# Attention and a SwiGLU feed-forward block on one core: preparing head pair 13 next to pair 12

## The chip, the core and the metric

The kernel runs on one core of a Trainium2 chip. The core has a matrix engine (TensorE, PE in the profile), a vector engine (VectorE, DVE), a scalar engine for activations (ScalarE, ACT), a general engine (GpSimd, POOL) and a queue engine (SyncE, SP), each with its own stream of instructions, and 16 DMA engines that all of them share. The metric is the time of one execution on the device, in microseconds (us); lower is better. The profile comes from one execution that was recorded.

## The reference

Softmax attention over 8 batches of 12 heads, sequence 448, head size 64, and behind it a feed-forward block on the 3584 tokens of width 768, with an inner width of 1536:

```python
scores = scale * np.matmul(q, k.transpose(0, 1, 3, 2))
attn = exp(scores - max) / (sum + 1e-09)
x = np.matmul(attn, v).transpose(0, 2, 1, 3).reshape(B * S, H * D)
g, val = x @ w_gate, x @ w_val
out = (g * sigmoid(g) * val) @ w_out
```

## The kernel before

**Pairs.** The attention is worked in 48 pairs of heads, six to a batch; two heads of 64 fill TensorE's 128 rows. A pair needs q and k with the head dimension on the partitions. Pairs 0 to 10 are transposed by TensorE. From pair NPE = 11 on, the float16 copies of q and k are laid side by side in a tile `qk16` by POOL, and a DMA transpose that SP issues writes them to `qkT`. From pair FULL = 12 on, the key rows are cut in three chunks of 128 and a remainder of 64 per head, so that the score matmuls use all 128 columns. `prep` (its branch for `pr >= FULL`, lines 188 to 203) does this for one pair: two memsets for the padding (L193, L194), a copy of the main k rows (L195), two of the remainder rows (L197), one of q (L198), and the transpose on SP (L200). There are three `qk16` buffers and five of `qkT`.

**Loads.** `load_qk16` issues the loads of q and k from POOL's queue, which also converts float32 to float16. With `n=2` it loads two pairs, with `n=1` one. From pair 12 on that is four DMAs: q (L127), main k rows (L136), and the remainder rows of each head (L138, twice). Pairs 12 and 13 are loaded together by the entry ("qk", 12) of the work queue `wq`, under pair 4. From pair 14 on each pair is loaded when the pair six before it (LA = 6) is entered. V is loaded in groups of three pairs: `load_v` with a memset (L165), two remainder loads (L167) and a main load (L171) for part 0, and one main load for the others. The gate and value weights (L185), and w_out in two halves (`wo`, L187, 1152 KB each), come through POOL's queue as well. The two halves of w_out are issued when pairs 6 and 7 are entered. All these DMAs take turns with eight completion semaphores: the ninth waits for the first to land.

**Order of work.** The order is written out by hand and each engine follows it. The main loop runs over visits. A visit issues the scores of two or three chunks (`qk`, TensorE matmul L275 and exponential L278 on ScalarE); from pair 12 on, a visit is one pair. Then it prepares a later pair: when pair `pr` is entered, `prep(pr + 3)` is called, and after it `load_qk16(pr + 6, 1)`. Then come the sums or the weighted values of an earlier pair (`reduce4`, L299), the V load of a later group, and a share of the feed-forward work: gate and value products (L362 or L365, in four column tiles when `tiled`), activation L381, the two vector steps L393 and L396, out-products (`op<-wo,hts`) and their copy L426. The remainder scores of a pair (`qk_rest`, tile `sr`) end its visit. The first out-products, those of the first feed-forward block, use the first half of w_out for its three row chunks and then the second half for the same chunks.

Around the change the visits go: pair 9 is entered, then pair 10 (within the next visit), pair 11, and from pair 12 on one pair per visit. So pair 12 is prepared under pair 9, pair 13 under pair 10, pair 14 under pair 11 and pair 15 under pair 12. Pair 14 is loaded under pair 8, pair 15 under pair 9, pair 16 under pair 10.

Of the kernel before, what the change touches and what calls it, by code (L numbers as in the profile page):

```python
# [19 lines left out]
NPE = 11  # L20
# [4 lines left out]
FULL = 12  # L25
# [3 lines left out]
def kernel(  # L29
# [19 lines left out]
    NPAIR = B * NHP  # L49
# [139 lines left out]
    def prep(pr):  # L189
        if pr >= FULL:  # L190
            rq, km, kr = raw[pr]
            qk16 = attp.tile([128, 2, NC, 2, D], FP16, tag="qk16", bufs=3, name="qk16")
            nc.gpsimd.memset(qk16[96:128, 1], 0.0)  # L193
            nc.gpsimd.memset(qk16[:, 0, 3], 0.0)  # L194
            nc.gpsimd.tensor_copy(qk16[:, 0, 0:3].rearrange("p c h d -> p h c d"), km)  # L195
            for hx in range(2):
                nc.gpsimd.tensor_copy(qk16[ts(hx, SR), 0, 3, hx], kr[ts(hx, SR)])  # L197
            nc.gpsimd.tensor_copy(qk16[0:P, 1].rearrange("p c h d -> p h c d"), rq)  # L198
            qkT[pr] = attp.tile([128, 2 * NC, 128], FP16, tag="qkT", name="qkT", bufs=5)
            nc.sync.dma_start_transpose(  # L200
                qkT[pr][:], qk16[:].rearrange("p t c h d -> p (t c h d)")
            )
            return None
        rq, rk = raw[pr]
        if pr == 0 or pr >= NPE:
            qk16 = attp.tile([128, 2, NC, 2, D], FP16, tag="qk16", bufs=3, name="qk16")[0:P]
            for t, src in enumerate((rq, rk)):
                dst = qk16[:, 1 - t].rearrange("p c h d -> p h c d")
                if pr == 0:
                    nc.vector.tensor_copy(dst[:, 0], src[:, 0])  # L210
                    nc.scalar.activation(dst[:, 1], src[:, 1], AF.Copy)
                else:
                    nc.gpsimd.tensor_copy(dst, src)
        qkT[pr] = attp.tile([128, 2 * NC, 128], FP16, tag="qkT", name="qkT", bufs=5)
        qkT[pr] = qkT[pr][:].rearrange("p c q -> p (c q)")[:, 0 : 2 * NC * P].rearrange(
            "p (c q) -> p c q", q=P
        )
        if pr >= NPE:
            nc.sync.dma_start_transpose(
                qkT[pr], qk16.rearrange("p t c h d -> p (t c h d)")  # L220
            )
            return None

        def turn0():
            for t in range(2):
                tp = ps_s.tile([128, 2, 512], FP32, tag="s", name="tp")
                for c in range(NC):
                    for hx in range(2):
                        nc.tensor.matmul(
                            tp[ts(hx, 64), c // 2, ds(c % 2 * P, P)],  # L230
                            lhsT=qk16[:, 1 - t, c, hx],
                            rhs=ident[:],
                            start=True,
                            stop=True,
                        )
                dst = qkT[pr][:, ts(1 - t, NC)].rearrange("p (a c) q -> p a (c q)", a=2)
                nc.vector.tensor_copy(dst[:, 0], tp[:, 0, 0 : 2 * P])
                nc.scalar.activation(dst[:, 1], tp[:, 1, 0 : 2 * P], AF.Copy)

        def turn():  # L240
            if pr < FIRST + 2:
                tp = ps_s.tile([128, 2 * NC, 256], FP16, tag="s", name="tp")
            else:
                tp = ps_f.tile([128, 2 * NC, 128], FP16, tag="f", name="tp")
            for t in range(2):
                for c in range(NC):
                    for hx in range(2):
                        src = raw[pr][t][:, hx, c, :]
                        nc.tensor.transpose(tp[ts(hx, 64), (1 - t) * NC + c, 0:P], src, ident[:])
            nc.vector.tensor_copy(qkT[pr], tp[:, :, 0:P])  # L250

        return turn if pr else turn0
# [10 lines left out]
    def qk(pr, c):  # L263
        if c == 0:
            E[pr] = ep.tile([128, 2 * NC * S], FP16, tag="E", name="E")
        t = qkT[pr]
        s = ps_s.tile([128, 2, 512], FP32, tag="s")
        full = pr >= FULL
        for hx in range(2):
            if full:  # L270
                lhsT, rhs = t[ts(hx, 64), c], t[ts(hx, 64), NC:, 0:P]
            else:
                lhsT = t[ts(hx, 64)].rearrange("p c q -> p (c q)")[:, c * P : c * P + 128]
                rhs = t[ts(hx, 64), NC:, :].rearrange("p c q -> p (c q)")
            nc.tensor.matmul(s[:, hx, 0:S], lhsT=lhsT, rhs=rhs, start=True, stop=True)  # L275
        m = 128 if full else P
        dst = (e_main if full else e_old)(pr)[:, c]
        nc.scalar.activation(dst, s[0:m, :, 0:S], AF.Exp, scale=sm_scale)  # L278
# [42 lines left out]
    def scaled(p0, t, acc):  # L321
        b, hp = divmod(p0, NHP)
        kk, bb = divmod(b, NB)
        if kk not in X:
            X[kk] = xp.tile([128, NCB, NB * S], FP16, tag="X", name="X")
        nc.vector.tensor_tensor(  # L326
            X[kk][:, hp + t, ts(bb, S)], acc[:, 0:S], R[p0][:], ALU.mult
        )
# [124 lines left out]
    with tc.manual_schedule():  # L453
# [47 lines left out]
        def add_block(i, visits):  # L501
            f1, f2, n = block(i)
            oq.extend(ffn2_wait)
            ffn2_wait.clear()
            fvq.extend([(f1, NCB * n / 2400.0)] * NFB)
            own = [(f2, NFB * OH / 2400.0)] * (2 * (n // 128))
            (oq if i == 0 else ffn2_wait).extend(own)
            count.update(visits=visits, fv=NFB, o=len(oq), at=0, more=NFB - visits)
# [21 lines left out]
        def run_budget(budget):  # L530
            while (fvq or oq) and budget > 0:
                budget -= run_fv() if fvq else run_o()
            return budget
# [68 lines left out]
        def product(kind, p0):  # L602
            if kind == "sums":
                pop_deferred(99)
                deferred.extend(recips(p0, sums(p0)))
            else:
                if kind == 0:
                    pop_deferred(99)
                scaled(p0, kind, pv(p0, kind))

        carry = 0.0
        for x, (chunks, todo) in enumerate(plan):
            for pr, c in chunks:
                qk(pr, c)
            end = min([y for y in adds if y > x] + [len(plan) + 1])
            if x == 0:
                for t in range(2):
                    scaled(p4, t, halves[t])
                add_block(0, end)
            turn2 = None  # L620
            entered = [pr for pr, c in chunks if c == 0]
            for pr in entered:
                if NPE <= pr + 3 < NPAIR:
                    prep(pr + 3)
                if 14 <= pr + LA < NPAIR:
                    load_qk16(pr + LA, 1)
            for pr, c in chunks:
                if c == 2 and pr < NPE - 2:
                    prep(pr + 2)()
            any_p = len(todo)  # L630
            if x in adds and x > 0:
                while todo:
                    product(*todo.pop(0)[1:])
                add_block(adds[x], end - x)
            while todo:
                product(*todo.pop(0)[1:])
            for pr in entered:
                if 4 <= pr // GP + 1 < NGRP:
                    load_v(pr // GP + 1, pr % GP)
                for w in wq.pop(pr, []):  # L640
                    emit(w)
            tiled[0] = bool(any_p) and (not chunks or chunks[0][0] >= TILED)
            rests.extend(pr for pr in entered if pr >= FULL)
            if adds[max(y for y in adds if y <= x)] < 2:
                carry = run_budget(left() / (end - x) + carry)
            else:
                at, n = count["at"], count["visits"]
                no = share(count["o"], at, n)
                nf = 1
                if no and count["more"] > 0:  # L650
                    o_left = sum(1 for y in range(at, n) if share(count["o"], y, n))
                    extra = -(-count["more"] // o_left)
                    nf += extra
                    count["more"] -= extra
                count["at"] += 1
                for y in range(nf):
                    if fvq:
                        run_fv()
                for _ in range(no):
                    run_o()  # L660
            run_rests()
            tiled[0] = False
# [36 lines left out]
```

## Time and profile before

| what | value |
|---|---|
| median of 6 runs | 460.84 us (460.3 to 462.8) |
| the profiled execution, its own time | 462.8 us |
| its span, first to last instruction | 461.0 us |
| mean granted TensorE clock | 0.993 |
| busy share of the span: PE, DVE, ACT, POOL | 97%, 51%, 50%, 52% |
| moved by DMA | 45.63 MB, 99 GB/s over the span |
| the two halves of w_out, issue to landing | 14.4 and 22.6 us |
| DMA transposes, issue to landing, shortest, median, longest | 3.4, 5.2, 12.2 us |

The page gives busy time by engine, the chain of work that ended last, and groups of instructions by source line. A timeline lists one engine's instructions in order: start, duration, line, tiles, and in brackets the idle time just before with what ended it. In the view of DMA, q0 is the queue of POOL's loads and q1 that of the transfers that SP issues.

### The profile page before, as it was taken

The numbers are of one execution on the slowest core, as the hardware profiler recorded it, in microseconds if no ns is written. First come the engines' busy times: TensorE is split into PE (matmuls) and PEld (weight loads), VectorE is DVE, ScalarE is ACT, GpSimd is POOL, SyncE is SP. The second block draws the span as 40 slices with busy tenths as digits, with TensorE's granted clock in tenths as the row PEclk, the third lists the DMA queues.
The fourth block names the chain that finished last, engine by engine and source line by source line (L and its number), as shares of the span: only waits on it lengthen the run. The fifth ranks groups of instructions, "written<-read, shape, count | busy, mean of one in ns | idle before, by whom it ended". The sixth has DMA issues, their size and how long they took to land.

```text
span 461.0 us, 17413 instructions
## 1 busy us (share of the span) xinstructions
PE 447.9 (97%) x7844; PEld 251.5 (55%) x7844; DVE 236.9 (51%) x375; ACT 231.4 (50%) x353; POOL 237.9 (52%) x472
## 2 busy tenths in 40 slices
PE   8899996999999999999999999999999999999996
PEld 3355554444456666555556656555556667544564
DVE  2765763267764563645636636446456456355200
ACT  6986574555555544544465465445544642222222
POOL 8554707999899979970589609990150000000000
PEclk9999999799999999999999999999999999999999
DMA  9999997897879889973479747973353101200133
GB/s 135 197 200 201 181 181 87 109 182 94 115 96 107 125 114 116 138 97 43 78 103 118 108 83 94 131 82 81 48 67 60 37 3 42 66 0 2 34 104 102
DMA packets 100618, 45.63 MB, mean 99 GB/s; under 512 B 71360, under 2 KB 97088, under 8 KB 100544
## 3 DMA queue, kind: packets, MB, share of 16 engines
q0 software_dynamic: 56320, 23.38, 43.9%
q1 hardware_dynamic: 44128, 21.09, 25.0%
q8 instruction: 61, 1.00, 1.0%
q14 instruction: 13, 0.11, 0.1%
q10 hardware_dynamic: 96, 0.05, 0.0%
HBM read 47.19 MB, written 11.01 MB: 126 GB/s over the span
## 4 chain that ended last, share of the span: by engine, by line
PE 83%; DMA 11%; DVE 1%; POOL 1%; ACT 1%; issue 1%; SPq 0%; DVEq 0%
PE vp L365 18%; PE gp L365 18%; PE op L365 16%; PE acc L299 11%; PE op L362 6%; PE s L275 6%; DMA wo<-in_moe_w_out_dram 5%; PE gp L362 4%; PE vp L362 4%; DMA wg<-in_moe_w_gate_dram 2%; DMA q<-in_q_dram 2%; PE sr L365 1%; DMA qkT<-qk 1%; ACT E L278 1%; DMA rk<-in_k_dram 1%
## 5 line engine op out<-in xcount | busy, mean ns | idle before, releaser
L278 ACT ACTIVATE E<-s 128x896 f16<-128x896 f32 (+1 forms) x156 | 131.6, 923 | 17.1 <-PE s L275 16.8
L365 PE MATMUL gp<-X,wg 128*32 128x384 f16 (+1 forms) x1824 | 99.6, 351 | 0.0
L365 PE MATMUL vp<-X,wv 128*32 128x384 f16 (+1 forms) x1824 | 99.3, 351 | 0.0
L393 DVE SCALAR_TENSOR_TENSOR t<-sg,gp 128x384 f32<-128x384 f32 (+1 forms) x96 | 58.5, 610 | 72.2 <-ACT sg L381 71.6
L365 PE MATMUL op<-wo,hts 128*32 128x384 f16 x1968 | 87.7, 329 | 0.4 <-issue 0.4
L426 ACT ACTIVATE osb<-op 128x384 f32<-128x384 f32 (+1 forms) x57 | 27.7, 486 | 117.9 <-PE op L365 94.2
L381 ACT ACTIVATE sg<-gp 128x384 f32<-128x384 f32 (+1 forms) x96 | 52.6, 547 | 62.6 <-PE gp L365 36.1
L350 DVE RECIPROCAL R<-ssb 128x112 f32<-128x112 f32 x92 | 73.8, 829 | 0.1
L365 PEld LDWEIGHTS <-hts 128*32 128x32 f16 x1968 | 57.1, 98 | 26.5 <-issue 2.4
L365 PEld LDWEIGHTS <-wg 128*32 128x32 f16 x1824 | 51.9, 97 | 35.3 <-issue 0.5
L365 PEld LDWEIGHTS <-wv 128*32 128x32 f16 x1824 | 51.9, 97 | 34.5 <-issue 1.6
L396 DVE SCALAR_TENSOR_TENSOR hts<-t,vp 128x384 f16<-128x384 f32 (+1 forms) x96 | 59.6, 621 | 10.8 <-DVE t L393 1.0
L326 DVE TENSOR_TENSOR X<-acc,R 128x448 f16<-128x448 f32 x48 | 29.7, 624 | 46.0 <-PE acc L299 42.3
L275 PE MATMUL s<-qkT 64*128 64x448 f16 x312 | 41.8, 357 | 7.1 <-DMA qkT<-qk 4.7
L138 POOL DMA_DIRECT2D k<-in_k_dram x70 | 38.2, 558 | 15.6 <-DMA wo<-in_moe_w_out_dram 14.1
L299 PE MATMUL acc<-E,vt 128*32 128x448 f16 (+1 forms) x768 | 45.7, 358 | 0.0
L347 DVE COPY ssb<-acc 128x448 f32<-128x448 f32 x23 | 14.4, 625 | 55.9 <-PE acc L299 55.9
L165 POOL MEMSET vt<- 128x384 f16 x12 | 5.3, 445 | 55.9 <-PE acc L299 55.9
L283 ACT ACTIVATE E<-sr 128x448 f16<-128x448 f32 x36 | 19.6, 544 | 24.7 <-PE sr L365 24.7
L127 POOL DMA_DIRECT2D q<-in_q_dram x42 | 28.6, 681 | 5.4 <-PE s L275 2.5
L299 PEld LDWEIGHTS <-vt 128*32 128x32 f16 (+1 forms) x768 | 18.6, 97 | 20.3 <-issue 8.7
L362 PE MATMUL op<-wo,hts 128*128 128x384 f16 (+1 forms) x192 | 29.6, 316 | 0.0
(53 smaller groups left out, 363.0 us busy)
## 6 DMA issues: line engine op xcount, KB each, us to landing
q<-in_q_dram POOLq DMA_DIRECT2D x37, 112.0 KB, 3.6
vt<-in_v_dram POOLq DMA_DIRECT2D x36, 96.0 KB, 3.4
k<-in_k_dram POOLq DMA_DIRECT2D x34, 96.0 KB, 4.4
out_dram<-osb SPq DMA_DIRECT2D x7, 336.0 KB, 3.2
wg<-in_moe_w_gate_dram POOLq DMA_DIRECT2D x8, 288.0 KB, 11.0
wv<-in_moe_w_val_dram POOLq DMA_DIRECT2D x8, 288.0 KB, 11.2
wo<-in_moe_w_out_dram POOLq DMA_DIRECT2D x2, 1152.0 KB, 18.5
out_dram<-osb SPq DMA_DIRECT2D x8, 288.0 KB, 3.0
```

The costliest lines, as they stand in the source:

```text
L127: nc.gpsimd.dma_start(q16[:, here], qf.rearrange("h (p c) d -> p h (c d)", c=NC))
L138: nc.gpsimd.dma_start(kr[ts(hx, SR), ds(h0 // 2, n)], kf[:, SM:].rearrange("(i t) p d -> t p i d", t=2)[hx],)
L275: nc.tensor.matmul(s[:, hx, 0:S], lhsT=lhsT, rhs=rhs, start=True, stop=True)
L278: nc.scalar.activation(dst, s[0:m, :, 0:S], AF.Exp, scale=sm_scale)
L299: nc.tensor.matmul(acc[ts(j, 32), 0:S], lhsT=weights(pr, hx, c), rhs=rhs, start=(c == 0), stop=(c == NC - 1),)
L326: nc.vector.tensor_tensor(X[kk][:, hp + t, ts(bb, S)], acc[:, 0:S], R[p0][:], ALU.mult)
L350: lambda i=i: nc.vector.reciprocal(rt[:, ts(i, P)], ssb[:, ts(i, P)]) for i in range(4)
L362: nc.tensor.matmul(dst, lhsT=lhsT, rhs=rhs, start=start, stop=stop)
L365: nc.tensor.matmul(dst[ts(j, 32), :], lhsT=lhsT[:, ts(j, 32)], rhs=rhs, start=start, stop=stop)
L381: nc.scalar.activation(sg[:, 0:n], gp[:, 0:n], AF.Tanh, scale=0.5)
L393: nc.vector.scalar_tensor_tensor(t1[:, 0:n], sg[:, 0:n], 1.0, gp[:, 0:n], ALU.add, ALU.mult)
L396: nc.vector.scalar_tensor_tensor(hts[:, fb, 0:n], t1[:, 0:n], 0.5 * HS, vp[:, 0:n], ALU.mult, ALU.mult)
```

## The change

When pair 9 is entered, pair 13 is prepared right behind pair 12, and no longer when pair 10 is entered. The loads of pair 15 follow behind both. Every other pair is prepared where it was. No engine gets an instruction more or less, and the order changes on POOL alone: the two memsets and four copies of pair 13 now stand between the copies of pair 12 and the four loads of pair 15. Before, these four loads and the four instructions of a V load (L165, L167 twice, L171) stood between them. SP's transposes keep their order.

```diff
             for pr in entered:
-                if NPE <= pr + 3 < NPAIR:
+                if NPE <= pr + 3 < NPAIR and pr + 3 != FULL + 1:
                     prep(pr + 3)
+                if pr + 3 == FULL:
+                    prep(FULL + 1)
                 if 14 <= pr + LA < NPAIR:
                     load_qk16(pr + LA, 1)
```

## The prediction

> **What bounds the kernel now.** I read the page first, then TensorE's timeline where its one long wait stands, then the queues behind that wait.
>
> The page (busy shares, the chain of waits, and the group of the wait):
>
> ```profile
> PE 447.9 (97%) x7844; PEld 251.5 (55%) x7844; DVE 236.9 (51%) x375; ACT 231.4 (50%) x353; POOL 237.9 (52%) x472
> ...
> PE 83%; DMA 11%; DVE 1%; POOL 1%; ACT 1%; issue 1%; SPq 0%; DVEq 0%
> ...
> L275 PE MATMUL s<-qkT 64*128 64x448 f16 x312 | 41.8, 357 | 7.1 <-DMA qkT<-qk 4.7
> ```
>
> TensorE (PE) is busy 97% of the span: whatever delays it, or saves it a wait, goes almost whole into the time. The third line names one wait of 4.7 us on a transposed copy. TensorE's timeline (start us, duration us, engine, line) shows it:
>
> ```profile
> 72.73 4.08 PE L365 MATMUL op<-wo,hts 128*32 128x384 f16 x96
> 76.62 0.38 PE L365 MATMUL sr<-qkT 128*32 128x448 f16 x4
> 81.69 1.30 PE L275 MATMUL s<-qkT 64*128 64x448 f16 x6 [4.69 <-DMA qkT<-qk]
> 82.92 1.69 PE L299 MATMUL acc<-E,vt 112*32 112x448 f16 x16
> 84.38 3.16 PE L365 MATMUL op<-wo,hts 128*32 128x384 f16 x48
> 87.37 0.36 PE L365 MATMUL sr<-qkT 128*32 128x448 f16 x4
> 87.67 0.74 PE L275 MATMUL s<-qkT 64*128 64x448 f16 x6
> ```
>
> By the order of the program the scores at 70.39 are pair 12's, at 81.69 pair 13's, at 87.67 pair 14's, at 95.34 pair 15's. Pair 13 is waited for from 77.0 to 81.69. After it the same six score matmuls last 1.30 us against 0.74: TensorE runs at half clock (the clock record has 0.5 from 79.66 for 6.83 us). From 81.69 to 87.67 pass 5.98 us; the same steps at full clock, from their own starts elsewhere (scores 0.67, P·V 0.77, 48 matmuls of the out-product 1.95, remainder scores 0.19), take 3.6. So the stall costs 4.7 + 2.4 = 7.1 us. That is the prize.
>
> POOL's timeline shows why pair 13 is late:
>
> ```profile
> 54.54 0.61 POOL L198 COPY qk<-q 112x512 f16<-112x512 f16 x1
> 55.09 0.67 POOL L127 DMA_DIRECT2D q<-in_q_dram  x1
> 55.75 0.73 POOL L136 DMA_DIRECT2D k<-in_k_dram  x1
> 61.87 0.54 POOL L138 DMA_DIRECT2D k<-in_k_dram  x1 [5.39 <-DMA wo<-in_moe_w_out_dram]
> 71.11 0.53 POOL L138 DMA_DIRECT2D k<-in_k_dram  x1 [8.70 <-DMA wo<-in_moe_w_out_dram]
> ...
> 74.38 0.52 POOL L193 MEMSET qk<- 32x512 f16 x1
> ...
> 76.13 0.61 POOL L198 COPY qk<-q 112x512 f16<-112x512 f16 x1
> ...
> 79.91 0.52 POOL L193 MEMSET qk<- 32x512 f16 x1
> ...
> 81.66 0.61 POOL L198 COPY qk<-q 112x512 f16<-112x512 f16 x1
> ```
>
> Pair 12 is prepared up to 55.1. Then come the four loads of pair 15; the last two reuse semaphores of the two halves of w_out and wait until these have landed (61.55 and 70.83: issued 47.15 and 48.17, landing after 14.4 and 22.6). Pair 13's copies stand behind them at 74.38, pair 14's at 79.91. SP's transposes follow the copies at once: issued 50.38, 55.17, 76.77, 82.30, 87.84 for pairs 11 to 15, landing after 10.5, 12.2, 4.9, 5.0, 5.6 us, so at 60.9, 67.4, 81.65, 87.3, 93.4. Pair 14's lands only 0.4 us before TensorE asks for it at 87.67. That is the next in line.
>
> **What the skill says.** "TensorE: Matmul & The Clock Gate", Part 1: TensorE falls to half clock after an idle window of about 3.4 us and returns after a busy one, the windows running free of the kernel. The trace agrees in size: 6.83 us is two such windows; here a window that still held 0.7 us of work sufficed to drop. "DMA: Bandwidth & Descriptors", Queues, rings and completion order: each DMA engine alternates packet by packet between the queues with work. The trace agrees, 370 packets against 368 below.
>
> **The change, part by part.** Nothing is added or removed. Pair 13's two memsets, four copies and transpose move ahead of the four loads of pair 15.
>
> *Copies, 2.36 us of POOL.* 0.52+0.20+0.50+0.52+0.61 = 2.35, and by the timeline from 74.33 to 76.69. They now run from 55.1 to 57.45. Their data was loaded with pair 12's (issued before 44, and copied from at 53.5 without a wait); the third qk16 buffer is free. The cover is the idle time of 5.39 us before 61.87, which shrinks to 3.0; were it gone, 2.36 us would be added to POOL's queue. Pair 15's first two loads slip 2.36 us, at no cost: they stand behind w_out in POOL's DMA queue and landed at 72.2 and 72.7 anyway, and pair 15 is copied after 85.
>
> *Transpose 13.* Issued at about 57.5, behind transpose 12. Transpose 11 landed at 60.9, 12 at 67.4: 6.4 us each under the weights' load. So 13 lands near 73.8, with 3 us to spare before 77.0. The 4.7 us wait goes.
>
> *What the transpose does to w_out.* DMA view of 68 to 70, with no transpose under way, then of 64 to 66 with transpose 12 (queue: packets, MB, share):
>
> ```profile
> q0 software_dynamic: 799, 0.37, 141.5%
> ```
>
> ```profile
> q0 software_dynamic: 370, 0.28, 90.2%
> q1 hardware_dynamic: 368, 0.09, 35.8%
> ```
>
> The loads drop from 0.37 to 0.28 MB per 2 us, and 62 to 64 has only 0.17, a standstill of nearly 1 us in mid-transpose. In its first 5 us (61 to 66) transpose 12 kept 0.04+0.20+0.09 = 0.33 MB of weights back, 1.8 us at the free rate. Transpose 13 now runs from 67.4, ahead of w_out's last 3.4 us. So w_out's second half lands later by d: 1.2 us without the standstill, 1.8 with it, 3 at the worst; not below 0, for a transpose on the same engines can't speed a load. I take 1.8: landing 72.6, just before TensorE asks at 72.73.
>
> *Pair 14.* Behind that landing POOL's chain is the old one less the copies of pair 13: rest load, memset, V loads, four loads of pair 16, V load, copies of pair 14. Its transpose is issued at 82.30 − 2.36 + d = 79.94 + d and lands 5.0 later: 84.94 + d = 86.7.
>
> *TensorE.* After 77.0 the 3.6 us of pair 13's visit run at full clock, so pair 14 is asked for at 80.6, not at 87.67. It waits from 80.6 to 86.7, 6.1 us instead of 4.7: the stall has not gone, it has moved on by one pair. The clock drops again; half clock costs between 1.2 (restart early in a window) and 2.6 us, 2.4 in this trace; I take 2.0. Pair 14 then begins in effect at 86.7 + 2.0 = 88.7 against 87.67.
>
> *Sum.* −2.36 (copies off POOL's chain) −0.37 (pair 14 had that slack) +1.8 (w_out later) +2.0 (half clock now after pair 14's landing, not ahead of it) = +1.1 us. Against the profiled span of 461.0 that gives 462.1; on the median of 460.84 it gives 461.9. (The profiled execution itself took 462.8, 1.8 over its span; the others 460.3 to 460.94.)
>
> *Next in line.* Pair 15: its transpose goes from 87.84 to about 87.3, landing by 93, asked for at 96. Pair 16's landed at 101.6 for a use at 102.3; POOL is no later and the use is. Nothing further waits.
>
> **The rivals.**
>
> *A, the forecast:* the wait moves to pair 14 and the sum is about zero: 460.84 − 1.4 to + 1.4, likeliest 461.9.
>
> *B, slower:* one mechanism, transpose 13 on the DMA engines while w_out's second half lands. At d = 3, with half clock at 2.4, the sum is +2.7 and the time 463.5; it decides from d of about 2.1. For it: the last DMA engine finished w_out at 70.83, most others by 69.5, so a laggard stretches; two transposes out of two had a standstill. Against it: most of w_out is in by 67.4.
>
> *C, a small gain:* d near 0.3 and the clock back after 1.2 us: −1.2 to −1.5, 459.3 to 459.6. For it: the bulk of w_out is early. Against: both queues alternate strictly while both have work.
>
> *D, the full prize:* the stall vanishes, 460.84 − 7.1 = 453.7. It needs pair 14 landed by 80.6, 4.3 us before the chain allows even with d = 0. Against it: POOL's order behind the w_out wait is unchanged.
>
> *E, the change doesn't do what it says:* transpose 13 lands after 77.0, because 12's delay is stretched too; a second wait is added before pair 14's, but pair 14 is still set by POOL: no more than about +0.5. It goes with A and B.
>
> **How the numbers follow.** Chances: A 0.47, B 0.38, C 0.11, D 0.04. About 0.3% (1.4 us) is what a measurement of this kernel can tell from no change. So faster 0.15 (C and D), same 0.47, slower 0.38. The ends d = 0 with 1.2 and d = 3 with 2.6 give −1.5 and +2.9; D at 0.04 stays outside. Range 459.3 to 463.8.
>
> **What would show it.** Right: no wait for pair 13; w_out's second half landing at 72 to 73.5; POOL's second rest load after 72; pair 14's transpose issued at 81 to 83; a wait of 5 to 7 us before pair 14's scores and half clock behind it. Wrong: a wait under 3 us there (C or D), w_out landing at 71 (d is 0), transpose 13 landing after 77 (E), or a further wait at pair 15 or 16.

## The result: no difference that counts, and the profile after

| | median, us | runs |
|---|---|---|
| kernel before | 461.87 (460.3 to 463.34) | 72 |
| changed kernel | 462.23 (461.38 to 464.1) | 34 |

The ratio is 1.0011, with a 95% interval of 1.0004 to 1.0017: half a microsecond slower, inside the 0.3% that I had called no change. (The six first runs of the kernel before had a median of 460.84; with 72 runs it is 461.87. So the forecast difference of +1.1 us is the figure to compare; that the absolute time came out near the forecast 461.9 says nothing.)

The profiled execution took 461.72 us with a span of 459.9. Its page, the lines that answer to those of before:

```profile
PE 446.9 (97%) x7844; PEld 251.4 (55%) x7844; DVE 236.9 (52%) x375; ACT 231.3 (50%) x353; POOL 238.0 (52%) x472
...
PE 81%; DMA 15%; POOL 3%; issue 1%; ACT 0%; POOLq 0%
...
L275 PE MATMUL s<-qkT 64*128 64x448 f16 x312 | 41.6, 356 | 6.9 <-DMA qkT<-qk 4.9
```

The last line is the whole story in short: 4.9 us of waiting for a transposed copy, where it was 4.7. TensorE's timeline shows for whom (start, duration, engine, line; in brackets the idle time before):

```profile
76.58 0.38 PE L365 MATMUL sr<-qkT 128*32 128x448 f16 x4
76.89 0.74 PE L275 MATMUL s<-qkT 64*128 64x448 f16 x6
77.56 0.94 PE L299 MATMUL acc<-E,vt 112*32 112x448 f16 x16
78.33 2.12 PE L365 MATMUL op<-wo,hts 128*32 128x384 f16 x48
80.28 0.36 PE L365 MATMUL sr<-qkT 128*32 128x448 f16 x4
85.51 1.08 PE L275 MATMUL s<-qkT 64*128 64x448 f16 x6 [4.87 <-DMA qkT<-qk]
86.52 1.69 PE L299 MATMUL acc<-E,ones 128*32 128x448 f16 x16
...
94.81 0.74 PE L275 MATMUL s<-qkT 64*128 64x448 f16 x6
```

Pair 13's scores follow at 76.89 without a wait and its visit runs at full clock. Pair 14's wait until 85.51, and behind them TensorE is at half clock. Pair 15 begins at 94.81; in the first profile of the kernel before it began at 95.34. (In the second profiles of the two kernels it was the other way round, 95.38 and 95.09.) POOL's timeline holds the reason:

```profile
57.77 0.61 POOL L198 COPY qk<-q 112x512 f16<-112x512 f16 x1
58.33 0.67 POOL L127 DMA_DIRECT2D q<-in_q_dram  x1
...
61.87 0.54 POOL L138 DMA_DIRECT2D k<-in_k_dram  x1 [2.15 <-DMA wo<-in_moe_w_out_dram]
71.72 0.53 POOL L138 DMA_DIRECT2D k<-in_k_dram  x1 [9.32 <-DMA wo<-in_moe_w_out_dram]
...
78.16 0.52 POOL L193 MEMSET qk<- 32x512 f16 x1
...
79.91 0.61 POOL L198 COPY qk<-q 112x512 f16<-112x512 f16 x1
```

Pair 13's copies end at 58.4 and are paid by the wait that stood there, which shrank from 5.39 to 2.15 us. The second wait for w_out is still there, 9.32 us where it was 8.70, and everything up to pair 14's copies stands behind it. They end at 80.5; the transpose is issued at 80.55 and lands 4.9 us later.

### The profile page after: what moved, and what is told of

It is laid out like the page before. It is cut to its first block, busy times and chain, and to the rows that moved or that the text cites. A ratio compares the mean times of both kernels' runs of the same rounds, so it can differ in the third digit from the quotient of the medians.

```text
span 459.9 us, 17411 instructions
## 1 busy us (share of the span) xinstructions
PE 446.9 (97%) x7844; PEld 251.4 (55%) x7844; DVE 236.9 (52%) x375; ACT 231.3 (50%) x353; POOL 238.0 (52%) x472
## 4 chain that ended last, share of the span: by engine, by line
PE 81%; DMA 15%; POOL 3%; issue 1%; ACT 0%; POOLq 0%
PE vp L365 18%; PE gp L365 18%; PE op L365 15%; PE acc L299 10%; PE op L362 6%; PE s L275 5%; DMA wo<-in_moe_w_out_dram 5%; DMA q<-in_q_dram 4%; PE gp L362 4%; PE vp L362 4%; DMA wv<-in_moe_w_val_dram 2%; DMA wg<-in_moe_w_gate_dram 2%; PE sr L365 1%; DMA qkT<-qk 1%; POOL q L127 1%
## 5 line engine op out<-in xcount | busy, mean ns | idle before, releaser
L365 PE MATMUL op<-wo,hts 128*32 128x384 f16 x1968 | 86.5, 326 | 0.0
L350 DVE RECIPROCAL R<-ssb 128x112 f32<-128x112 f32 x92 | 73.8, 829 | 0.1
L165 POOL MEMSET vt<- 128x384 f16 x12 | 5.4, 449 | 56.8 <-PE acc L299 56.8
```

Of the source, the lines that this page charges most:

```text
L350: lambda i=i: nc.vector.reciprocal(rt[:, ts(i, P)], ssb[:, ts(i, P)]) for i in range(4)
L365: nc.tensor.matmul(dst[ts(j, 32), :], lhsT=lhsT[:, ts(j, 32)], rhs=rhs, start=start, stop=stop)
```

## The experiments

Two of the profiles repeat the kernels themselves; ratios are to the kernel before on the same chip, with their 95% intervals.

### Pair 14 one visit earlier too

```diff
-                if NPE <= pr + 3 < NPAIR and pr + 3 != FULL + 1:
+                if NPE <= pr + 3 < NPAIR and pr + 3 not in (FULL + 1, FULL + 2):
                     prep(pr + 3)
-                if pr + 3 == FULL:
-                    prep(FULL + 1)
+                if pr + 3 in (FULL, FULL + 1):
+                    prep(pr + 4)
```

> The changed kernel, and pair 14 too is copied one visit earlier, ahead of the loads of pair 16. Theory (POOL's order behind the w_out wait sets pair 14): its copies start at 74.9 instead of 78.2, the transpose lands near 82.2, the wait for pair 14 falls from 4.9 to about 1.7 us; pairs 15 and 16 then are next to be late by 1 to 2 us each, since POOL is no further ahead for them; time 2 to 4 us under the kernel before. Rival 1 (the loss is the collision of transpose 13 with w_out on the DMA engines): w_out lands as late as in the changed kernel, and the order of POOL behind it matters little; time within 1 us of the kernel before. Rival 2 (only the half clock matters): the wait falls but the clock still drops; 1 to 2 us under.

Measured: 459.01 us, ratio 0.9929 (0.9904 to 0.9955), 2.8 us under the kernel before by the medians. TensorE's score groups in its timeline:

```profile
81.90 0.74 PE L275 MATMUL s<-qkT 64*128 64x448 f16 x6 [1.51 <-DMA qkT<-qk]
...
90.48 0.74 PE L275 MATMUL s<-qkT 64*128 64x448 f16 x6 [0.84 <-DMA qkT<-qk]
...
98.08 0.74 PE L275 MATMUL s<-qkT 64*128 64x448 f16 x6 [0.61 <-DMA qkT<-qk]
```

The wait for pair 14 fell from 4.87 to 1.51 us, and pairs 15 and 16, never waited for before, now are. The clock stayed full. Their transposes landed within half a microsecond of where they did in the changed kernel (90.5 and 98.0 against 90.9 and 98.4), but TensorE asked 5.2 and 4.3 us earlier. So the order of POOL's work sets the wait, and the lateness is passed from pair to pair. Rival 1 fails as the sole cause: w_out landed hardly earlier here (22.3 us after its issue against 22.5).

### Every pair from 14 on one visit earlier

The edit, against the changed kernel:

```diff
-                if NPE <= pr + 3 < NPAIR and pr + 3 != FULL + 1:
+                if NPE <= pr + 3 <= FULL:
                     prep(pr + 3)
-                if pr + 3 == FULL:
-                    prep(FULL + 1)
+                if FULL < pr + 4 < NPAIR:
+                    prep(pr + 4)
```

> The changed kernel with every pair from 14 on copied one visit earlier, ahead of the loads that follow. Theory (the wait is handed from pair to pair by POOL's order): the 1.5 us wait for pair 14 of the run with pair 14 alone stays, those for pairs 15 and 16 (0.84 and 0.61 there) go; time 1 to 2 us under that run's 459.0. Rival (it is the DMA engines): waits of about a microsecond stay at pairs 15 and 16 because the transposes themselves land later; time as in that run.

Measured: 458.81 us, ratio 0.9920 (0.9891 to 0.9950). The scores of pairs 14, 15 and 16 in its timeline:

```profile
82.08 0.74 PE L275 MATMUL s<-qkT 64*128 64x448 f16 x6 [1.67 <-DMA qkT<-qk]
...
89.75 0.74 PE L275 MATMUL s<-qkT 64*128 64x448 f16 x6
...
96.67 0.74 PE L275 MATMUL s<-qkT 64*128 64x448 f16 x6
```

The waits for pairs 15 and 16 are gone and 1.67 us at pair 14 stay, as the theory has it; but the medians of five runs each differ by 0.2 us only. The trace confirms the mechanism; the medians don't confirm its size. The granted clock explains part of that (see the table at the end of this section).

### The collision alone: no transpose of pair 13

```diff
+            if pr == FULL + 1:
+                qkT[pr] = qkT[FULL]
+                return None
             qkT[pr] = attp.tile([128, 2 * NC, 128], FP16, tag="qkT", name="qkT", bufs=5)
```

> The changed kernel without the transpose of pair 13: its scores read pair 12's transposed tile, so pair 13's result is left out; its copies on POOL stay. Theory (order of POOL): w_out's second half lands 0.6 to 1.8 us earlier, pair 14's wait shrinks by as much from 4.9 but stays over 3 us with half clock behind it; time 0.5 to 1.8 us under the changed kernel. Rival 1 (collision): without the collision the wait for pair 14 is nearly gone and the time is 4 us or more under the kernel before.

Measured: 459.95 us, ratio 0.9962 (0.9950 to 0.9974), 0.49% or 2.3 us under the changed kernel by the ratios, a little more than I gave. POOL's second wait for w_out, and TensorE's for pair 14 (three source lines lower here):

```profile
70.05 0.53 POOL L138 DMA_DIRECT2D k<-in_k_dram  x1 [7.55 <-DMA wo<-in_moe_w_out_dram]
```

```profile
83.83 1.25 PE L278 MATMUL s<-qkT 64*128 64x448 f16 x6 [3.03 <-DMA qkT<-qk]
```

POOL is released 1.67 us earlier, and the wait for pair 14 is 1.84 us shorter. So the transpose does cost w_out about that much, but 3.0 us of the wait stay without it: the collision is the smaller part, POOL's order the larger.

How the loads lose is seen in the DMA view of 67.5 to 70 (queue: packets, MB, share), first in the changed kernel, then in the second profile of the kernel before, where nothing transposes then:

```profile
q0 software_dynamic: 437, 0.29, 100.9%
q1 hardware_dynamic: 449, 0.11, 66.5%
```

```profile
q0 software_dynamic: 1057, 0.43, 139.3%
```

The two queues' packets are about as many (437 and 449), and POOL's queue moves 0.29 MB in place of 0.43. (In the other profile of each kernel it is 0.31 and 0.47.)

### The half clock alone

```diff
+            if chunks and chunks[0] == (FULL + 2, 0):
+                dummy(20)
             for pr, c in chunks:
                 qk(pr, c)
```

> The changed kernel with 20 idle-filling matmuls (512 columns, 4.3 us at full clock) on TensorE just ahead of pair 14's scores, where it waits. Theory: they fill the wait, pair 14 starts at the same time (85.5 in the trace), the clock stays full, and the time falls by the half-clock term of my sum, 1.2 to 2.6 us, likeliest 1.7, to about 460.5. Rival (the clock costs nothing, TensorE is not the bound behind the wait): no difference to the changed kernel.

Measured: 460.15 us, ratio 0.9967 (0.9951 to 0.9984). That is 0.44% or 2.0 us under the changed kernel.

```profile
80.97 4.48 PE L105 MATMUL wp<-warm 128*128 128x512 f16 x20 [0.41 <-ACT osb L426]
85.63 0.74 PE L275 MATMUL s<-qkT 64*128 64x448 f16 x6 [0.19 <-DMA qkT<-qk]
```

Pair 14 starts no earlier (85.63), but its matmuls take 0.74 us at once. Useless work in the wait is worth 2.0 us by the ratios: the half-clock term of the sum.

The same in the kernel before, ahead of pair 13 (the condition reads FULL + 1):

> The kernel before with 20 idle-filling matmuls (512 columns, 4.3 us at full clock) on TensorE just ahead of pair 13's scores, where it waits. Full clock behind pair 13's wait would bring pair 14's scores forward by 2.4 us, but pair 14's transpose had 0.4 us to spare in the first profile of the kernel before and 1.9 in the second. If the half clock there was mostly hidden behind pair 14's landing, as my sum says: gain 0.4 us and a new wait of 1 to 2 us for pair 14. If it was paid in full: gain 1.9 to 2.4 us and no wait for pair 14.

Measured: 460.37 us, ratio 0.9969 (0.9955 to 0.9983), a gain of 1.4 us, between the two readings.

```profile
81.81 0.74 PE L275 MATMUL s<-qkT 64*128 64x448 f16 x6
...
86.38 0.74 PE L275 MATMUL s<-qkT 64*128 64x448 f16 x6 [0.81 <-ACT E L283]
```

Pair 14's transpose landed at 86.33 here, so the idle time before 86.38 belongs to it, though the profile names ScalarE. In this kernel, then, a part of the half clock was hidden behind pair 14's landing; in the changed kernel none was. Why the gain falls between the two readings is seen in the table at the end of this section: both of them occur.

### The load of w_out out of the way

```diff
-            7: [("o", 1)],
+            9: [("o", 1)],
```

> The changed kernel with the load of w_out's second half issued two pairs later, behind the loads of pair 15 and the V load. Theory (POOL stood behind the rest load of pair 15, which waited for w_out): that wait goes, pair 14 is copied before 70, neither pair 13 nor pair 14 is waited for, and the whole 7 us come in, less what TensorE waits for w_out at 72.7 if it lands later than that (0 to 1.5 us); time 454 to 456.5. Rival 1 (collision on the DMA engines): the same bytes and transposes compete, w_out lands 2 us or more after 72.7, the gain is under 4 us.

Measured: 461.84 us, ratio 0.9997 (0.9977 to 1.0017). I was wrong on the size: nothing was gained, as rival 1 had it.

```profile
76.85 5.37 PE L365 MATMUL op<-wo,hts 128*32 128x384 f16 x96 [4.19 <-DMA wo<-in_moe_w_out_dram]
```

Neither pair 13 nor 14 is waited for any more, but w_out is. POOL came to issue the load at 66.47, later than I had assumed (a V load waited 1.25 us for one of pair 14's), and it took 10.3 us to land. How much of these 10.3 us is the collision that rival 1 named, and how much the late issue behind other loads, no run here separates. The stall of four to five microseconds changed its name a second time, and 3.41 us of half clock followed it.

### Pair 14 ahead of the V load as well

The first V load of group 4 is issued behind the copies of pair 14:

```diff
                 if FULL < pr + 4 < NPAIR:
                     prep(pr + 4)
+                if pr + 4 == FULL + 2:
+                    load_v(4, 0)
...
-                if 4 <= pr // GP + 1 < NGRP:
+                if 4 <= pr // GP + 1 < NGRP and pr + 3 != FULL:
                     load_v(pr // GP + 1, pr % GP)
```

> As the run with all pairs from 14 on one visit earlier, and the first V load of group 4 is issued behind the copies of pair 14, not ahead of them. Theory: pair 14's copies start when its loads have landed (73.2 to 73.6), its transpose lands near 80.5, just as TensorE asks for it; no wait over 0.5 us is left, the clock stays full, and the whole 7 us of the stall come in: 454 to 456. Rival (DMA engines): pair 14's loads and transpose are held back by the transposes, a wait of 1 us or more stays, 457 or more.

Measured: 455.72 us, ratio 0.9866 (0.9839 to 0.9893). This beats both kernels. POOL, then TensorE:

```profile
71.73 0.53 POOL L138 DMA_DIRECT2D k<-in_k_dram  x1 [9.30 <-DMA wo<-in_moe_w_out_dram]
72.29 0.52 POOL L193 MEMSET qk<- 32x512 f16 x1
...
74.75 0.41 POOL L165 MEMSET vt<- 128x384 f16 x1
```

```profile
80.64 0.74 PE L275 MATMUL s<-qkT 64*128 64x448 f16 x6
```

POOL waits for w_out as long as in the changed kernel (9.30 against 9.32 us), but now pair 14 is the first thing it does behind that wait. Pair 14's transpose lands at 79.7, ahead of 80.64. No wait of more than 0.2 us for a transpose is left on TensorE, and the clock stays full.

### The change undone in that kernel

```diff
+                if pr + 3 == FULL + 1:
+                    prep(pr + 3)
-                if FULL < pr + 4 < NPAIR:
+                if FULL + 1 < pr + 4 < NPAIR:
                     prep(pr + 4)
```

> The run with pair 14 ahead of the V load, with the change itself undone: pair 13 is copied when pair 10 is entered, just ahead of pair 14. Theory: w_out lands 1 to 1.7 us earlier without transpose 13 beside it, pair 13's transpose lands near 79, TensorE waits 2 to 2.7 us for it, [...]and pair 14 is not waited for; time 2 to 3 us over that run: that is what the change is worth once pair 14 is out of the way. Rival (the change is worth nothing in any order): no difference to that run.

Measured: 455.64 us, ratio 0.9864 (0.9833 to 0.9896): no difference to the run with the change (four runs each). My expectation of 2 to 3 us fell. POOL, SP's transpose of pair 13 from issue to landing, and TensorE's scores of pairs 13 and 14:

```profile
70.30 0.53 POOL L138 DMA_DIRECT2D k<-in_k_dram  x1 [7.41 <-DMA wo<-in_moe_w_out_dram]
70.87 0.52 POOL L193 MEMSET qk<- 32x512 f16 x1
...
73.29 0.52 POOL L193 MEMSET qk<- 32x512 f16 x1
```

```profile
DMA to landing us min/median/max: 3.0/3.0/3.0
```

```profile
77.21 0.74 PE L275 MATMUL s<-qkT 64*128 64x448 f16 x6
80.89 0.74 PE L275 MATMUL s<-qkT 64*128 64x448 f16 x6
```

Without transpose 13 beside it w_out landed earlier (POOL goes on at 70.30, not 71.73), and with no loads issued right behind the copies transpose 13 took 3.0 us, not the 4.9 I had carried over. It landed at 76.3, ahead of 77.2. (Pairs 15 and 16 wait 0.27 and 0.44 us here.) So in the better order the change is worth nothing: pair 13 is in time when its copies come directly behind the w_out wait, ahead of the V load.

### Both kernels once more

> The kernel before, a second profile. Its w_out's second half took 22.6 us from issue to landing in the first, its last DMA engine 1.3 us behind the next. If that laggard is chance, here it lands after 20.5 to 21.5 us and pair 13's wait is 1 us shorter; if it belongs to the kernel, again after 22 to 23 us with a wait of 4.7 us.

```profile
69.47 0.53 POOL L138 DMA_DIRECT2D k<-in_k_dram  x1 [7.57 <-DMA wo<-in_moe_w_out_dram]
```

```profile
80.97 1.30 PE L275 MATMUL s<-qkT 64*128 64x448 f16 x6 [4.28 <-DMA qkT<-qk]
```

POOL was held until 69.47 here, not 71.11: w_out took 20.5 us, not 22.6. Without an early transpose 13 it took 20.5, 20.5, 20.9 and 21.3 us in four profiles and 22.6 in the first alone; with it, 22.3 to 23.2 in six. So the laggard that the prediction started from was chance, one profile in five. The wait was only 0.4 us shorter, though, not 1 us: here transpose 13 took 5.8 us to land, not 4.9, and TensorE asked 0.3 us earlier.

> The changed kernel, a second profile, with times beside the kernel before on the same chip. From pair 12's scores to pair 15's it took 24.5 us in the first profile, with half clock for 3.4 us. If the half clock depends on where the clock's window happens to stand, this stretch varies between 24 and 26.5 us with half clock for 3.4 or 6.8 us; if it belongs to the kernel, 24.5 again. Time by the recorded runs: 0.5 us over the kernel before.

Times: ratio 1.0014 (0.9999 to 1.0030), the same half microsecond. From the table of stretches of this second profile (us, busy times, then granted clock, DMA share, GB/s):

```profile
84.00:86.00 2.00, 0.52 (x4) 0.28 (x6) 0.00 (x0) 0.00 (x0) 1.82 (x6) 0.50 1.16 130
88.00:90.00 2.00, 2.00 (x28) 0.82 (x20) 0.68 (x2) 0.68 (x1) 1.70 (x5) 0.50 1.28 197
```

and of the first:

```profile
84.00:86.00 2.00, 0.49 (x4) 0.21 (x6) 0.00 (x0) 0.03 (x1) 1.82 (x6) 0.94 1.07 120
88.00:90.00 2.00, 2.00 (x36) 0.95 (x32) 1.06 (x2) 0.51 (x1) 1.70 (x4) 0.70 1.26 201
```

With the same wait (4.86 and 4.87 us) the clock was halved for 6.83 us in one and 3.41 in the other. From pair 14's scores to pair 15's passed 9.90 and 9.30 us; 7.67 is full speed, so 2.2 and 1.6 us were lost. By the clock record the half clock began at 85.76 in the first profile, just behind the wait, and its one window of 3.41 us was filled with work. In the second it began at 83.32, inside the wait; that window held 1.25 us of matmuls, and a second one followed. So for the same wait the place of the window decides.

The runs that were timed with the experiments, and those of the changed kernel, have their mean granted clock on record, and it tells the number of such windows: 0.996 in the three profiles that show one, 0.991 to 0.993 in the three that show two, 0.998 to 1.0 in the six that show none. I sorted the runs by it afterwards (0.995 counted with one window). Medians in us, in brackets the number of runs; several chips are mixed:

| | no window | one | two |
|---|---|---|---|
| kernel before | | 460.80 (28) | 462.35 (42) |
| changed kernel | | 461.72 (15) | 462.39 (32) |
| changed, no transpose of pair 13 | 457.82 (1) | 459.95 (17) | 461.75 (2) |
| pair 14 earlier too | 459.01 (5) | | |
| every pair from 14 earlier | 456.76 (2) | 458.90 (3) | |
| changed, wait filled | 460.15 (11) | | |
| before, wait filled | 460.37 (13) | | |

(One run of the kernel before, 462.39 us with a clock of 1.0, is left out.) With one window the change costs 0.9 us by these medians, with two it costs nothing; the half microsecond is a mix of both. Filling the wait gains 1.6 us over one window and 2.2 over two in the changed kernel, as the two traces have it. In the kernel before it gains 0.4 and 2.0 (on the one chip where both were timed 0.4 and 2.1): the two readings of that experiment both occur, and 1.4 is their mix. With one window on both sides, leaving out transpose 13 is worth 1.8 us, close to the 1.67 and 1.84 of the trace, where the ratios gave 2.3. And every pair from 14 on earlier is about 2 us under pair 14 alone where neither has a window, though on two runs only; three of its five runs had a window, and no trace shows where.

## Why the prediction was right, point by point

**The wait moves to pair 14.** Right, in place and cause. No wait for pair 13, POOL's second wait for w_out in place, pair 14's copies behind it. Pair 14 was asked for at 80.64 (85.51 − 4.87; forecast 80.6).

**Copies in POOL's idle time.** Right: 2.4 us, taken from the first w_out wait (5.39 to 2.15; the queue also ran 0.8 us later in this profile).

**Transpose 13.** It landed at 73.4 (forecast 73.8), 15.0 us after its issue at 58.40.

**w_out later by d.** The second half of w_out from its issue (start, duration) in the two profiles of the kernel before, in the run without transpose 13 and in the changed kernel:

```profile
48.17 22.65 DMA wo<-in_moe_w_out_dram
48.74 20.45 DMA wo<-in_moe_w_out_dram
49.23 20.54 DMA wo<-in_moe_w_out_dram
48.98 22.45 DMA wo<-in_moe_w_out_dram
```

The mechanism was right and the size nearly: POOL waits 1.67 us longer than in the run without transpose 13. The mean is 22.7 us in the six profiles with it and 20.8 in four of the five without, 1.9 apart; with the late first profile counted it is 21.2, and 1.6 apart. Forecast 1.8. What was off is its base. I added d to a landing that was itself late by chance, by 22.65 − 20.8 = 1.8 us; that the load was issued 0.8 us later in the new profile hid a part. So w_out landed at 71.4, not 72.6; transpose 14 was issued at 80.55, not 81.7, landed at 85.46, not 86.7; and the wait was 4.87 us, not 6.1.

**The slack of pair 14.** This term holds the same chance once more: where w_out landed earlier, in the second profile of the kernel before, pair 14 had 1.9 us to spare (landing 85.5, use 87.42), not 0.37. With 1.9 the sum reads −2.36 − 1.9 + 1.8 + 2.2 = −0.3 us, an estimate for runs with two windows, where the table has 0.0. For the 0.9 us of the runs with one window, pair 14 would have to have next to no slack in the kernel before; no profile shows such a run, so this stays open. I also took the half clock from a profile with two windows (462.8 us) and the median from six runs of which five, at 460.3 to 460.94, lie where one window puts them. The measured +0.5 us is a mix of two cases that the sum didn't tell apart; that +1.1 came out so near it is in part luck.

**Half clock.** Right: 2.0 us forecast, 2.0 measured by filling the wait, 1.6 and 2.2 in the traces. The 2.4 us that I read from the trace before are nearer 2.3, since pair 13's visit at full clock took 3.7 us in the changed kernel (76.89 to 80.6), not 3.6. "TensorE: Matmul & The Clock Gate", Part 1, says that the windows run free of the kernel; the two profiles of one kernel, with one and two windows of 3.41 us, agree.

**Next in line.** Pairs 15 and 16 were not waited for, as said. They had 3.9 and 3.3 us to spare (landed at 90.9 and 98.4, used at 94.81 and 101.73); the first experiment uses that up.

**The signs.** No wait for pair 13 and half clock behind pair 14's came as said. The four figures that I had named as signs all fell just short of their ranges: w_out at 71.4 (72 to 73.5), POOL's second rest load at 71.72 (after 72), transpose 14's issue at 80.55 (81 to 83), the wait of 4.87 us (5 to 7). All four hang on the late base of w_out.

**Rivals.** B needed a d of about 2.1 and fell short with 1.6 to 1.9. C and E did not happen. D was given 0.04 because POOL's order was unchanged; with the order changed it came in, 6.7 us against the changed kernel (0.9866 against 1.0011), which is the wait of 4.87 plus about 1.9 of half clock.

## What to carry to other kernels

When a wait is removed by moving one item ahead in a queue, ask when the next item is due and what the queue still stands behind: here a load that waited for a slow load's semaphore held the queue, and each pair pulled forward handed the same wait on. Put the work that feeds the busy engine first behind such a hold, and the loads that are needed later second; that was worth 1.3%, with or without the change. And take a landing time for a sum from more than one profile when one DMA engine of sixteen decides it; the same holds for the clock, where one or two windows of half speed moved the kernel before by about 1.5 us, more than the change did.

## What the runs showed of the hardware that I had not expected

- The one transpose with no loads right behind it (pair 13's with the change undone) landed in 3.0 us; those from 74 to 90 us with loads issued in the same stretch took 4.6 to 5.9, one 6.9.
- The third transpose in flight held SP's queue: its issue took 5.3 us (58.40 to 63.7), and 5.2 to 5.5 in the other five traces where it runs beside both halves of w_out, against 1.2 to 1.8 for the other transposes in the profiles of the two kernels. Nothing else stood in SP's queue then, so it cost nothing here.
- Transposes beside the w_out load met a near standstill of both queues, of 0.7 to 1.0 us: in the trace's DMA packets from 55.7 and 63.2 in the first profile of the kernel before, from 63.2 and 69.7 in that of the changed kernel, where a fifth at 56.2 was shorter (0.3). All came about the end of a fetch of instructions, one packet of some 0.9 to 1.1 us. The fetch at 68 to 69 is a comparison: the six traces in which transpose 13 is still under way then have a standstill behind it, the five without an early transpose 13 have none. That the fetch and the transpose together cause it was not tried.
